# Sliding and dilated attention with a squared-ReLU block: v without overlapping key blocks, halos copied by ScalarE, larger DMA rows for dilated q k and for the results

## The chip, the cores and the metric

The kernel runs on one NeuronCore of a Trainium2 chip, as one launch. The metric is the device time of that launch in microseconds (us). The core has five engines that run their own instruction queues in order: TensorE (PE, matmuls, with its weight loads shown as PEld), VectorE (DVE), ScalarE (ACT), GpSimd (POOL) and SyncE (SP). DMA transfers are issued here from SP and from POOL.

## The reference

```python
# q, k, v: (8 batches, 8 heads, 576 positions, 64) float32
scores = scale * np.matmul(q, k.transpose(0, 1, 3, 2))
rel = pos[:, None] - pos[None, :]
mask_plain = (rel >= 0) & (rel < 32)                          # heads 0-3
mask_dil = (rel >= 0) & (rel < 32 * 4) & (rel % 4 == 0)       # heads 4-7
attn = softmax(where(mask, scores, -1e9))
x = np.matmul(attn, v).transpose(0, 2, 1, 3).reshape(4608, 512)
g = np.maximum(x @ w_in, 0.0) ** 2                            # w_in: 512 x 2048
out = g @ w_out                                               # w_out: 2048 x 512
```

A query of a sliding head (0 to 3) sees itself and the 31 positions before it. A query of a dilated head (4 to 7) sees every fourth position, 32 in all; sorted by position modulo 4 (a "class"), it is again a window of 32 within its class of 144.

## The kernel before

**Attention, per batch.** The sliding heads work in 6 blocks of QB = 96 queries, each against 128 keys: its own 96 and the PADP = 32 before them. The dilated heads work per class in 2 blocks of QD = 72 queries, each against 128 keys: its own 72 and the PADD = 56 before them. `s_sliding` and `s_dilated` compute scores as keys x queries into PSUM; `softmax` takes the exponential on ACT (L509) into `AT` and multiplies with a 0/1 mask on DVE (L510, `maskp` and `maskd`). `av_sliding` and `av_dilated` multiply `AT` with v (L567, L581), where a column of ones beside v gives the sum of the row; `normalize` divides on DVE (L552, L553). `x_sliding` and `x_dilated` transpose the result on PE, and ACT copies it into `xT` (L602, L620).

**v.** Since every key block has 128 rows and the blocks overlap, v is loaded with the overlap: `load_sliding_v` (L124) issues six DMAs from SP into `sv` (float32, 128 partitions, blocks outermost), each with the block's 32 rows of halo; `load_dilated_v` (L133) issues two into `sd`, of 72 and of 128 rows. POOL then casts them to float16 (`cast_sliding_v` L166, three copies; `cast_dilated_v` L170, four copies) into `vp` and `vd`, of which there are two each, for even and odd batches. For batch 0 two small DVE copies (L662, L664) stand before the loads, so that these start after the q k loads; for batch 1 two POOL copies (L687, L688) do that. `sv` and `sd` exist once.

**q and k.** For batches 0 and 1 they are loaded by POOL's DMAs (`load_qk`) and transposed on PE (`t_sliding`, `t_dilated`). From batch 2 on the DMA engines transpose. Sliding: load (`load_sliding_qk`), re-ordering copy `nr` (`by_token`, L119, on POOL for batch 2, on DVE afterwards), a store to a DRAM tile `dp` (L194), transposes from there into `QKTp` (L202). Dilated: a copy from DRAM to DRAM with a cast to float16 into `dd` (`keep_dilated_qk`, L183), whose rows are padded from 256 to 320 elements, and transposes from there into `QKTd` (L206). Before the loads for the next batch POOL waits for the transposes (`after_transposes`, L211).

**Hidden layer and output.** The 4608 tokens are worked in 9 chunks of 512. `mm1_gen` makes 16 hidden blocks per chunk: 4 matmuls (L269), Relu on ACT into `rt` (L292), square on DVE into `g` (L293). Chunks 0 and 1 use plain products (`mm2`, L403). Chunks 2 to 8 use one level of Strassen (`mm2_strassen_gen`): seven products of half width, whose operands DVE prepares as sums (`gs` L302 and L303, `g` L372, `wt` L319). ACT takes a product out of PSUM (`take`, L359), DVE adds another one (`add`, L370), and SP stores each of the four 256x256 quarters of the chunk with its own DMA (`leave`, L362), in rows of 1 KB.

**The order** is written by hand. The attention of batch b is emitted step by step, and between its steps `pump(n)` emits n pieces of the hidden layer of chunk b - 1, so PE, ACT and DVE each see attention and hidden layer interleaved in a fixed order. `attn_scores` and `attn_values` hold the steps; hooks in them emit the transfers for the next batch. Batch 0 is written out at L661 to L712, with filler matmuls (`fill_gen`) between its steps.

Of the kernel before, what the change touches and what calls it, by code (L numbers as in the profile page):

```python
# [17 lines left out]
def kernel(  # L18
# [32 lines left out]
    PADD = P - QD  # L51
    KPAD = 64
    DPAD = 64
# [9 lines left out]
    otp = ctx.enter_context(tc.tile_pool(name="otp", bufs=5))  # L63
# [27 lines left out]
    sv = stg.tile([P, NB, HH, D], FP32, name="sv")  # L91
# [32 lines left out]
    def load_sliding_v(b):  # L124
        for m in range(NB):
            lo = QB * m - PADP
            p0 = PADP if m == 0 else 0
            nc.sync.dma_start(
                out=sv[p0:P, m, :, :],
                in_=v[b, 0:HH, lo + p0 : lo + P, :].transpose([1, 0, 2]),  # L130
            )

    def load_dilated_v(b, eng):  # L133
        vv = v[b, HH:H].rearrange("h (i c) d -> i h (c d)", c=DIL)
        eng.dma_start(out=sd[PADD:P, 0, :, :], in_=vv[0:QD])
        eng.dma_start(out=sd[:, 1, :, :], in_=vv[QD - PADD : CL])

# [28 lines left out]
    def cast_sliding_v(b, ms=range(0, NB, 2)):  # L166
        for m in ms:
            nc.gpsimd.tensor_copy(vp[b % 2][:, m : m + 2, :, 0:D], sv[:, m : m + 2, :, :])  # L168

    def cast_dilated_v(b):  # L170
        for t in range(2):
            for c in range(0, DIL, 2):
                nc.gpsimd.tensor_copy(  # L173
                    vd[b % 2][:, t, c : c + 2, :, 0:D],
                    sd[:, t, :, D * c : D * (c + 2)].rearrange("p h (c d) -> p c h d", d=D),
                )

# [5 lines left out]
    def keep_dilated_qk(b):  # L183
        d = dpool.tile([2, HH * CL, DIL * D + DPAD], FP16, name=f"dd{b}", tag="dd")
        for i, src in ((1, k), (0, q)):
            nc.gpsimd.dma_start(
                out=d[i, :, 0 : DIL * D], in_=src[b, HH:H].rearrange("h (i c) d -> (h i) (c d)", c=DIL)
# [16 lines left out]
    def transpose_dilated(b, dd):  # L204
        for i in (1, 0):
            nc.sync.dma_start_transpose(out=QKTd[b % 2][:, i, :, KPAD:], in_=dd[i, :, 0 : DIL * D])  # L206
# [10 lines left out]
    nc.vector.memset(sv[0:PADP, 0, :, :], 0.0)  # L217
# [12 lines left out]
    for m, w, pad in ((maskp, QB, PADP), (maskd, QD, PADD)):  # L230
# [7 lines left out]
            m.rearrange("p (n w) -> p n w", w=w),  # L238
            lo_[:, 0:w].unsqueeze(1).to_broadcast([P, UW // w, w]),
            hi_[:, 0:w].unsqueeze(1).to_broadcast([P, UW // w, w]),  # L240
        )
    nc.vector.memset(AT[:, :, UW:640], 0.0)
    for r in range(2):
# [8 lines left out]
            scalar1=-PADD + 0.5,  # L252
# [71 lines left out]
    def mm2_strassen_gen(c, g):  # L324
# [32 lines left out]
        def take(what):  # L357
            ot = otp.tile([P, 2, HM], FP32, name=f"o{what}{c}", tag="ot")
# [3 lines left out]
        def leave(ot, i, j):  # L362
            t0 = c * TOKC + HTOK * i
            nc.sync.dma_start(
                out=out[t0 : t0 + HTOK, HM * j : HM * (j + 1)].rearrange("(t p) m -> p t m", p=P),
                in_=ot,
# [4 lines left out]

        nc.vector.tensor_sub(g[:, 0:HF, HTOK:], g[:, 0:HF, 0:HTOK], g[:, 0:HF, HTOK:])  # L372
        yield from product(A, gq(0, 0), wq(0, 0))
        o11 = take("u")
# [4 lines left out]
        o21 = take("v")  # L379
# [5 lines left out]
        o22 = take("w")  # L385
        add(o22, Bk)
        leave(o22, 1, 1)
# [3 lines left out]
        leave(o11, 0, 0)  # L391
        yield
        yield from product(A, sq(1), wq(1, 1))
        o12 = take("x")
        leave(o12, 0, 1)
# [3 lines left out]
        leave(o21, 1, 0)  # L399
# [10 lines left out]

    def store(c, t, po):
        ot = otp.tile([P, DM], FP32, name=f"ot{c}_{t}", tag="ot")
# [116 lines left out]
    def s_dilated(b, g):  # L529
        tiles = [pa(f"pz{b}_{g}_{h}") for h in range(2)]  # L530
        for h, ps in enumerate(tiles):
            for a in range(2):
                for t in range(2):
                    q0 = KPAD + (2 * g + h) * CL + QD * t
                    for e in range(2):
# [4 lines left out]
                            QKTd[b % 2][r, 1, a, q0 - PADD : q0 - PADD + P],  # L540
# [84 lines left out]
    def attn_scores(b, gap, less=0, hooks={}):  # L625
# [5 lines left out]
        for g in range(2):  # L631
            s_dilated(b, g)
            if 2 + g in hooks:
                hooks[2 + g]()
            pump(gap - less)

    def attn_values(b, gap, wide=False, hooks={}):
        xs = []
        for mp in range(3):
            xs.append(av_sliding(b, mp))  # L640
            if 4 + mp in hooks:
                hooks[4 + mp]()
            pump(gap)
        x_sliding(b, 0, xs, wide)
        pump(gap)
# [151 lines left out]
```

## Time and profile before

| what | value |
|---|---|
| median of 11 runs | 315.65 us (313.05 to 318.95) |
| the profiled execution | 316.13 us |
| its span, first to last instruction | 314.1 us |
| granted TensorE clock | 1.000 |
| PE busy | 291.6 us (93%) |
| DVE busy | 210.2 us (67%) |
| ACT busy | 165.0 us (53%) |
| POOL busy | 76.4 us (24%) |
| DMA | 82801 packets, 46.73 MB, mean 149 GB/s |
| DMA packets under 512 B | 54352 |
| loads of v | sv 40 x 128 KB and 8 x 96 KB, sd 8 x 512 KB and 8 x 288 KB |

A line of the profile names the line of the code, the engine, the operation, and "out<-in" by the names of the tiles. In a timeline the first column is the start and the second the busy time in us; "x2" says how many instructions were merged; the bracket at the end tells how long the engine was idle before and what ended that. In a list of waits the numbers are the total in us, how many times, and the longest. A busy PE is not always PE at full rate, since its matmuls are pipelined and may wait inside.

### The profile page before, as it was taken

To read this page: it belongs to the slowest core of one execution; us is meant where nothing else is said; L and a number is where in the kernel's file an instruction comes from. 1 tells how busy PE (TensorE), PEld (TensorE's weight loads), DVE (VectorE), ACT (ScalarE), POOL (GpSimd) and SP (SyncE) were. 2 spreads that over 40 slices of the span, in tenths; PEclk is the share of its full clock that TensorE was granted. 3 is DMA by queue.
4 is the path that set the end of the run, shared out by engine and by line. 5 is a ranking of instruction groups with operands and counts; after the bars stand their busy time and mean duration, and the time that the engine had idled before them with its cause. 6 is when DMAs were issued, how large, how long until landed. Compare 5 with 4: busy or idle time off the path is not lost.

```text
span 314.1 us, 7145 instructions
## 1 busy us (share of the span) xinstructions
PE 291.6 (93%) x2874; PEld 195.4 (62%) x2874; DVE 210.2 (67%) x429; ACT 165.0 (53%) x286; POOL 76.4 (24%) x114
## 2 busy tenths in 40 slices
PE   1878998996999989998999999999999999999994
PEld 1444554453555558755798968557845885685583
DVE  5774448476852899479937993799469944734652
ACT  2736645566535942495239623872287336525620
POOL 4444018403320657022530514060000000000000
PEclk9999999999999999999999999999999999999999
DMA  7799997999999998999689977987310030012003
GB/s 125 160 228 214 205 201 130 195 192 205 206 172 201 293 219 159 229 179 222 168 171 215 247 150 101 261 203 151 102 35 0 2 102 33 0 38 100 3 0 134
DMA packets 82801, 46.73 MB, mean 149 GB/s; under 512 B 54352, under 2 KB 79952, under 8 KB 82768
## 3 DMA queue, kind: packets, MB, share of 16 engines
q1 hardware_dynamic: 68512, 31.60, 43.2%
q0 software_dynamic: 14256, 14.68, 28.8%
q8 instruction: 22, 0.36, 0.5%
q14 instruction: 11, 0.09, 0.1%
HBM read 39.85 MB, written 16.52 MB: 179 GB/s over the span
## 4 chain that ended last, share of the span: by engine, by line
PE 61%; DVE 19%; DMA 7%; ACT 5%; issue 2%; SPq 2%; POOL 1%; POOLq 0%; DVEq 0%
PE ph L269 24%; PE pa L346 12%; PE po L403 8%; PE pb L346 7%; DVE g L293 5%; ACT AT L509 3%; PE pc L346 3%; DVE x_p L553 3%; DMA sd<-in_v_dram 3%; DMA ns<-in_q_dram 2%; DVE AT L510 2%; DVE gs L303 2%; ACT rt L292 2%; DVE gs L302 2%; PE paw L581 2%
## 5 line engine op out<-in xcount | busy, mean ns | idle before, releaser
L269 PE MATMUL ph<-xT,wi 128*128 128x512 f16 (+1 forms) x640 | 133.4, 359 | 0.7 <-ACT xT L620 0.7
L292 ACT ACTIVATE rt<-ph 128x512 f16<-128x512 f32 x144 | 86.2, 615 | 45.4 <-PE ph L269 40.1
L269 PEld LDWEIGHTS <-wi 128*128 128x128 f16 x640 | 68.6, 114 | 46.8 <-issue 0.8
L293 DVE TENSOR_TENSOR g<-rt 128x512 f16<-128x512 f16 x144 | 64.1, 453 | 42.4 <-ACT rt L292 41.3
L346 PEld LDWEIGHTS <-g 128*128 128x128 f16 x448 | 42.3, 98 | 7.1 <-DVE g L372 1.4
L168 POOL CAST vp<-sv 128x512 f16<-128x512 f32 x24 | 17.1, 712 | 82.9 <-DMA sv<-in_v_dram 58.7
L346 PEld LDWEIGHTS <-gs 128*128 128x128 f16 x336 | 31.4, 98 | 5.4 <-DVE gs L303 2.0
L403 PE MATMUL po<-wo,g 128*128 128x512 f16 x128 | 33.1, 379 | 0.0
L173 POOL CAST vd<-sd 128x512 f16<-128x512 f32 x32 | 27.8, 905 | 11.4 <-DMA sd<-in_v_dram 8.9
L346 PE MATMUL pa<-wt,gs 128*128 128x256 f16 x224 | 29.1, 273 | 0.9 <-DVE gs L303 0.6
L346 PE MATMUL pb<-wt,g 128*128 128x256 f16 x224 | 27.7, 273 | 0.6 <-DVE g L372 0.6
L553 DVE TENSOR_TENSOR x_d<-paw,rcp_d 72x512 f16<-72x512 f32 x32 | 22.0, 686 | 1.1
L509 ACT ACTIVATE AT<-pz 128x576 f16<-128x576 f32 x32 | 20.0, 710 | 2.2 <-PE pz L538 2.0
L510 DVE TENSOR_TENSOR AT<-AT,maskp 128x576 f16<-128x576 f16 x32 | 16.4, 521 | 7.0 <-ACT AT L509 4.9
L509 ACT ACTIVATE AT<-ps 128x576 f16<-128x576 f32 x32 | 19.2, 661 | 3.4 <-PE ps L519 3.3
L620 ACT COPY xT<-py 128x576 f16<-128x576 f16 x16 | 10.2, 641 | 17.2 <-PE py L614 17.0
L510 DVE TENSOR_TENSOR AT<-AT,maskd 128x576 f16<-128x576 f16 x32 | 17.0, 548 | 3.1 <-ACT AT L509 1.5
L602 ACT COPY xT<-px 128x576 f16<-128x576 f16 x16 | 10.2, 639 | 14.3 <-PE px L596 13.7
L370 DVE TENSOR_TENSOR ov<-pb,ov 128x512 f32<-128x512 f32 x7 | 4.8, 692 | 18.2 <-PE pb L346 18.2
L553 DVE TENSOR_TENSOR x_p<-pav,rcp_p 96x512 f16<-96x512 f32 x24 | 16.5, 687 | 0.8
L581 PEld LDWEIGHTS <-AT 128*128 128x128 f16 x256 | 11.7, 98 | 6.7 <-issue 1.7
L403 PEld LDWEIGHTS <-g 128*128 128x128 f16 x128 | 10.4, 98 | 8.0
(81 smaller groups left out, 284.6 us busy)
## 6 DMA issues: line engine op xcount, KB each, us to landing
sv<-in_v_dram SPq DMA_DIRECT2D x40, 128.0 KB, 6.5
sd<-in_v_dram SPq DMA_DIRECT2D x8, 512.0 KB, 7.3
dp<-nr SPq DMA_DIRECT2D x12, 288.0 KB, 5.1
ns<-in_k_dram POOLq DMA_DIRECT2D x8, 288.0 KB, 5.4
ns<-in_q_dram POOLq DMA_DIRECT2D x8, 288.0 KB, 6.9
sd<-in_v_dram SPq DMA_DIRECT2D x8, 288.0 KB
wo<-in_moe_w_out_dram POOLq DMA_DIRECT2D x4, 512.0 KB, 10.2
out_dram<-ow SPq DMA_DIRECT2D x7, 256.0 KB
```

Of the source, the lines that this page charges most:

```text
L168: nc.gpsimd.tensor_copy(vp[b % 2][:, m : m + 2, :, 0:D], sv[:, m : m + 2, :, :])
L173: nc.gpsimd.tensor_copy(vd[b % 2][:, t, c : c + 2, :, 0:D], sd[:, t, :, D * c : D * (c + 2)].rearrange("p h (c d) -> p c h d", d=D),)
L269: nc.tensor.matmul(ph[:, t0:t1], wi4[ffc // 4][:, dmk, :, ffc % 4], xT[:, dmk, x0 : x0 + t1 - t0], start=(dmk == 0 and t0 == 0), stop=(dmk ...
L292: nc.scalar.activation(rt, ph[:], ACTF.Relu)
L293: nc.vector.tensor_mul(g[:, ffc, :], rt, rt)
L346: nc.tensor.matmul(banks[bank][:, t], a(k, t), b(k), start=(new and t == 0 and k == 0), stop=(k == HF - 1), skip_group_check=True,)
L403: nc.tensor.matmul(po, g[:, ffc, t * P : (t + 1) * P], wo[ffc // 4][:, ffc % 4, :], start=(ffc == 0), stop=(ffc == NFF - 1),)
L509: nc.scalar.activation(AT[:, u, 0:UW], ps[:, :, 0 : UW // 2], ACTF.Exp, scale=scale)
L510: nc.vector.tensor_mul(AT[:, u, 0:UW], AT[:, u, 0:UW], mask)
L553: nc.vector.tensor_tensor(out=x[0:w], in0=pv[:, :, :, 0:D], in1=rcp[0:w].unsqueeze(3).to_broadcast([w, 2, HH, D]), op=ALU.mult,)
L581: nc.tensor.matmul(pav[:, e, h * (D + 2) : h * (D + 2) + D + 1], AT[:, 4 + h, off : off + P], vd[b % 2][:, t, 2 * a + e, h, 0 : D + 1], st ...
L602: nc.scalar.copy(xT[:, 0:2, t0 : t0 + 288], px[:, 0:UW].rearrange("x (c t) -> x c t", c=2),)
```

## The change

It has three parts.

1. v is loaded without overlap. A sliding block loads only its own 96 rows, into partitions 32 to 127 of `sv`, whose layout is now head, block, element; from batch 1 on this takes two DMAs (two heads each) instead of six. The dilated heads now have key blocks of 80 and 64 own rows (`OWND`), and the padding differs per block (`PADD = (48, 56)`), so each of two DMAs loads own rows only. POOL casts as before (the second dilated block on 64 partitions only). What the overlap brought is then copied on chip by ACT, from the end of one block to the start of the next: `halo_sliding` (three per batch, 32 partitions, 256, 512 and 512 elements) and `halo_dilated` (two per batch, 64 partitions, 512 elements). They stand in ACT's order behind the dilated scores and between the steps of `attn_values`. The rows of `sv` that no DMA writes any more are set to 0 once, by one more memset on DVE ahead of L662; `maskd` is made in two halves, since its two blocks differ.
2. `dd` has no padding any more, and the copy into it reads 16 positions (4 KB) at a time and writes 2 KB, where it read 1 KB and wrote 512 B.
3. The two quarters of the same tokens share a tile of full width, and `leave` stores both in one DMA with 2-KB rows; the last chunk still stores quarters. The pool of these tiles has 3 buffers of twice the size instead of 5.

```diff
-    PADD = P - QD
+    PADD = (48, P - QD)
+    OWND = (CL - 64, 64)
...
-    otp = ctx.enter_context(tc.tile_pool(name="otp", bufs=5))
+    otp = ctx.enter_context(tc.tile_pool(name="otp", bufs=3))
...
-    sv = stg.tile([P, NB, HH, D], FP32, name="sv")
+    sv = stg.tile([P, HH, NB, D], FP32, name="sv")
...
     def load_sliding_v(b):
-        for m in range(NB):
-            lo = QB * m - PADP
-            p0 = PADP if m == 0 else 0
-            nc.sync.dma_start(
-                out=sv[p0:P, m, :, :],
-                in_=v[b, 0:HH, lo + p0 : lo + P, :].transpose([1, 0, 2]),
-            )
+        vv = v[b, 0:HH].rearrange("h (m p) d -> p h m d", p=QB)
+        if b == 0:
+            for m in range(NB):
+                nc.sync.dma_start(out=sv[PADP:P, :, m, :], in_=vv[:, :, m, :])
+        else:
+            for h in (0, 2):
+                nc.sync.dma_start(out=sv[PADP:P, h : h + 2], in_=vv[:, h : h + 2])
...
     def load_dilated_v(b, eng):
         vv = v[b, HH:H].rearrange("h (i c) d -> i h (c d)", c=DIL)
-        eng.dma_start(out=sd[PADD:P, 0, :, :], in_=vv[0:QD])
-        eng.dma_start(out=sd[:, 1, :, :], in_=vv[QD - PADD : CL])
+        i0 = 0
+        for t in range(2):
+            eng.dma_start(out=sd[P - OWND[t] : P, t, :, :], in_=vv[i0 : i0 + OWND[t]])
+            i0 += OWND[t]
...
+    def halo_sliding(b, mp):
+        m0, m1 = max(1, 2 * mp), 2 * mp + 2
+        nc.scalar.copy(
+            vp[b % 2][0:PADP, m0:m1, :, 0:D], vp[b % 2][P - PADP : P, m0 - 1 : m1 - 1, :, 0:D]
+        )
+
+    def halo_dilated(b, c):
+        nc.scalar.copy(
+            vd[b % 2][0:64, 1, c : c + 2, :, 0:D], vd[b % 2][64:P, 0, c : c + 2, :, 0:D]
+        )
...
-        d = dpool.tile([2, HH * CL, DIL * D + DPAD], FP16, name=f"dd{b}", tag="dd")
+        d = dpool.tile([2, HH * CL, DIL * D], FP16, name=f"dd{b}", tag="dd")
         for i, src in ((1, k), (0, q)):
             nc.gpsimd.dma_start(
-                out=d[i, :, 0 : DIL * D], in_=src[b, HH:H].rearrange("h (i c) d -> (h i) (c d)", c=DIL)
+                out=d[i].rearrange("(r i) x -> r (i x)", i=4),
+                in_=src[b, HH:H].rearrange("h (r i) d -> (h r) (i d)", i=16),
+                max_dma_last_dim=4096,
             )
...
-    for m, w, pad in ((maskp, QB, PADP), (maskd, QD, PADD)):
+    md = maskd.rearrange("p (n t w) -> p n t w", t=2, w=QD)
+    for m, w, pad in (
+        (maskp.rearrange("p (n w) -> p n w", w=QB), QB, PADP),
+        (md[:, :, 0], QD, PADD[0]),
+        (md[:, :, 1], QD, PADD[1]),
+    ):
...
+    nc.vector.memset(sv[0:PADP, :, 1:NB, :], 0.0)
     nc.vector.memset(AT[:, :, UW:640], 0.0)
...
         take(upper, 1)
-        leave(o12, 0, 1)
+        leave(upper, 0, (1,) if last else (0, 1))
...
             s_dilated(b, g)
             if 2 + g in hooks:
                 hooks[2 + g]()
+            if g:
+                halo_sliding(b, 0)
             pump(gap - less)
...
             xs.append(av_sliding(b, mp))
+            if mp < 2:
+                halo_sliding(b, mp + 1)
+            else:
+                halo_dilated(b, 0)
...
         x_sliding(b, 0, xs, wide)
+        halo_dilated(b, 2)
         pump(gap)
```

In batch 0, which is written out, `halo_sliding(0, 0)` stands behind the sliding scores and ahead of `t_dilated`, `halo_sliding(0, 1)` behind `t_dilated`, and the other three behind the dilated scores.

## The prediction

> **What bounds the kernel now.** I read the page, then PE's waits, the busy time by stage, and the order of time at three places. PE is busy 291.6 of the 314.1 us span. So I first ask where PE waits at all. In the list of waits for PE alone (us in total, times, longest), these three matter:
>
> ```profile
> PE pav L567 <- DVE x_p L553: 2.8, 3, 1.5
> PE ps L519 <- DMA QKTp<-dp: 2.5, 1, 2.5
> PE paw L581 <- POOL vd L173: 1.6, 1, 1.6
> ...
> ```
>
> After the start-up nothing else reaches 1 us, so less DMA traffic can only buy these few waits. The stages confirm it (us, then PE, PEld, DVE, ACT, POOL busy; clock; DMA share; GB/s):
>
> ```profile
> 62.00:97.00 35.00, 32.52 (x270) 17.28 (x269) 21.81 (x47) 18.92 (x33) 8.02 (x14) 1.00 1.06 189
> 97.00:131.00 34.00, 32.28 (x323) 22.27 (x322) 26.00 (x48) 18.91 (x34) 15.93 (x19) 1.00 1.01 219
> 162.50:195.00 32.50, 31.78 (x382) 28.13 (x381) 24.98 (x49) 17.86 (x32) 10.28 (x14) 1.00 0.93 176
> 227.00:258.00 31.00, 31.00 (x319) 21.91 (x318) 22.79 (x48) 17.86 (x32) 0.00 (x0) 1.00 0.11 36
> ```
>
> The DMA engines are full up to about 195 us, but the stage with almost no DMA still takes 31.0 us, all of it PE. The middle stages are only 0.5 to 3 us above that. From 258 us on PE never waits, and that part is not changed except for wider stores.
>
> **Start-up, to the first full matmul of the hidden layer at 25.75 us.**
>
> ```profile
> 7.36 0.16 DVE L664 CAST sd<-ns 64x2 f32<-64x2 f16 x1
> 7.47 3.80 SPq L128 DMA_DIRECT2D sv<-in_v_dram  x6
> 7.54 1.42 DVE L164 COPY QKTp<-pt 128x576 f16<-128x576 f16 x2
> ...
> 13.58 0.38 SPq L136 DMA_DIRECT2D sd<-in_v_dram  x1
> ...
> 21.79 1.18 POOL L173 CAST vd<-sd 128x512 f16<-128x512 f32 x2 [3.14 <-DMA sd<-in_v_dram]
> ...
> 25.75 1.46 PE L269 MATMUL ph<-xT,wi 128*128 128x512 f16 x6 [0.73 <-ACT xT L620]
> ```
>
> DVE works without a pause from 4.08 us to these copies, and both the v load (gated by L662 and L664) and the scores (which need QKTp) stand behind it. The change puts more there: a memset of sv over 1280 elements of 32 partitions, and the dilated mask in two halves. The memset rows are 0.27 us for 256 elements and 0.91 us for 1024, so 0.83 ns an element and 1.13 us. The maskd triple (L231, L234, L237) took 0.80 us; two triples of half width come to about 2 x 0.62 = 1.24, so 0.44 more. Everything behind moves by 1.57 us. Bounds: 0 if a transfer turns out to be what the scores wait for, 2.0 us if the halves cost like whole masks.
>
> Against this, v(0) is 1152 KB instead of 1536 KB. The second dilated piece falls from 512 to 256 KB; it was issued at 13.58 and landed 8.15 us later, beside the 2 MB (as stored) of wi. Even started 1.57 us later it should land by 20 us. Then the cast wait (1.6 us on PE, 1.13 us on DVE) goes, and what is late next is DVE's row of x_d, at its own pace. Worth about 1.1 us. The first ACT halo stands ahead of ACT's two QKTd copies and waits for POOL's cast of the first two key blocks; the DVE halves of those copies ended 0.4 us after ACT's (13.88 against 13.47), which covers its 0.4 us. The second fits in ACT's 1.0 us gap before the dilated exps. The other three stand before the xT copies, whose reader (mm1) is later. Start-up net: **+0.5 us** (-1.0 to +2.5).
>
> **Batch 2, the 2.5 us wait of PE at 74.77 us.**
>
> ```profile
> 54.09 0.66 POOL L186 DMA_DIRECT2D dd<-in_q_dram  x1
> 57.84 2.11 POOL L119 COPY nr<-ns 128x2304 f16<-128x2304 f16 x1 [3.08 <-DMA ns<-in_q_dram]
> 62.68 6.85 SPq L206 DMA_TRANSPOSE QKTd<-dd  x2
> 69.63 3.14 SPq L202 DMA_TRANSPOSE QKTp<-dp  x2
> ...
> 74.77 0.43 PE L519 MATMUL ps<-QKTp 64*128 64x96 f16 x12 [2.48 <-DMA QKTp<-dp]
> ```
>
> SP issues the dilated transposes first, and the second of them starts at 66.20, about when dd of q lands (12 us after its issue); the sliding ones queue behind. Two parts of the change shorten this. POOL issues ns(2) and dd(2) only after its v(1) casts, which end at 52.2 and hang on v(1) landing. Up to there the queues carry 2 x 384 KB less, at 205 GB/s 3.7 us. And dd itself: the trace's packet records have 1152 packets of 512 B a batch at 61 ns, over 16 engines 4.4 us; the new copy writes 288 of 2 KB, and 2-KB packets of that queue took 174 ns, so 3.1 us. QKTp should be there 4 to 5 us earlier and the whole wait go. At 72.3 us PE has its next operands, and DVE was idle too, so nothing takes its place: **-2.4 us** (0 to -2.5). POOL's v casts stay as long: the dilated ones already read a permuted sd at the same 611 ns minimum as the sliding ones, and 64 partitions cost like 128.
>
> The padding of dd goes too (rows of 512 instead of 640 B). Here the row comes first: dp has unpadded 512-B rows, and its transposes land in 3.7 us, dd's padded ones in 3.8. A rule of the Trainium skill, "DMA: Bandwidth & Descriptors", section "Latency and other measured facts", speaks against it: row pitches at large powers of two fall from 207 to 103 GB/s, and padding brings the rate back. If that held here, each dilated transpose would take some 7.6 us and batch 2 keep its wait (2.4 us lost). The rule was measured from 512 KiB pitch up, and dp's row is near: I take nothing.
>
> **The other DMA waits.** In chunk 3 DVE stood 0.99 us at 141.59 for ns of batch 5, and PE then waited 1.0 us on x_p. That load runs beside v(5), now a quarter smaller, and follows dd and the transposes: -0.8 us (0 to -1.0). In chunk 2 PE's 1.5 us at 115.5 comes from DVE, whose mask multiplies took 1.65 us for two beside POOL's casts, and 1.00 elsewhere. The casts come some 3 us earlier, but the next batch's move into the same stretch: -0.5 us (+0.5 to -1.5). Stores in 2-KB rows: 6 x 1024 packets at 59 ns become 3072 at 85, some 1 us of DMA time a chunk; nobody waits for a store, and three otp buffers of twice the size are reused 12 us or more after their store is issued: 0.
>
> **What is added: five ACT copies a batch.** No row has ACT copying SBUF to SBUF. The nearest are COPY out<-PSUM 128x512 at 587 ns and 128x576 at 640: 0.83 ns an element, so 0.59 us for 512 and 0.38 for 256, in all 2.7 us a batch, 22 us of ACT. Bounds 0.45 (a shorter start on SBUF) and 0.735 us (the re-ordering copy QKTd<-pd). The sum by average says nothing (ACT is at 53%); the place does, in the stage where PE never waits:
>
> ```profile
> 237.23 1.22 ACT L292 ACTIVATE rt<-ph 128x512 f16<-128x512 f32 x2
> ...
> 238.82 0.60 ACT L292 ACTIVATE rt<-ph 128x512 f16<-128x512 f32 x1 [0.37 <-PE ph L269]
> ...
> 239.06 0.42 PE L567 MATMUL pav<-vp,AT 128*128 128x65 f16 x8
> ```
>
> ACT is gapless to 238.45. The halo for blocks 0 and 1 goes in at 237.25, ends at 237.6, and only the second half of the first pav (from 237.7) needs it: no wait. The two rt then end at 238.8, the next halo at 239.4, and its pav wants to start at 239.06: PE waits 0.4 us. Queued behind it is the next rt, and behind that DVE's g; the third halo ends at 240.6, before its pav. The rt of the last two hidden blocks come some 0.5 us later; gs, which needs them, had 0.68 us of room (246.42 against 247.10). So +0.4 in chunk 6; in chunks 2 to 5 the same wait is partly covered, since PE later waits for DVE anyway: 0.25 each; batch 1 about 0.2, batch 2, where ACT has room, 0.1. Sum **+1.7 us** (0.5 to 6).
>
> **Sum.** 0.5 - 2.4 - 0.8 - 0.5 + 1.7 = -1.5, say -1.4 us. The profiled execution took 316.13 us (span 314.1 and 2.0 around it), so 314.7 there; the median of the runs, 315.65, is 0.5 lower: **314.2 us**. A difference of 0.5%, 1.6 us, is about what can be told from none.
>
> **Rivals.** *More comes free* (0.27): start-up gains 1.0 us since the DVE delay is absorbed, and all waits for DVE shrink with the earlier casts: 1.0 + 2.4 + 1.0 + 1.2, less 1.1 for ACT, is -4.5: 311.1 us. For it: by the packet records the change saves 5120 packets of 256 B at 21.6 ns, 1792 of 1 KB at 59 ns, and the dd and store shares above, some 27 us over 16 engines, of the 226 us (72% of the span) that both queues take. Against it: DVE's work is not less.
>
> *ACT becomes late* (0.20), slower. The halos take 0.735 us or more and push rt, so DVE's g and gs come late where PE already waits for gs (0.5 us in chunk 4). Each of chunks 2 to 5 then pays 0.5 at pav and 0.5 at gs, chunk 6 pays 1.2, batches 1 and 2 0.8: 6.0 instead of 1.7, so 318.5 us. It outweighs all gains once the halos cost over 3.1 us of PE in all. Against it: idle ACT of 0.27 to 0.52 us before most rt.
>
> *Nothing nets* (0.08): the dd copies land no earlier, because their reads share full queues, and batch 2 keeps its wait; 2.4 lost of the gains, with ACT at its lower bound (1.2 less): -0.2, 315.5 us.
>
> The forecast has 0.45. About half of it lies over 0.5% faster: faster 0.46, within 0.34, slower 0.20. The range 310.8 to 317.9 takes in the first rival and the start-up's upper bound and leaves out most of the late-ACT case.
>
> **What would show it.** Right: no PE wait on QKTp at batch 2, dd landing well under 8.8 and 11.0 us, halos near 0.59 us, the first full ph at 26.2 us, and a wait of pav on an ACT copy of some 0.3 us a chunk. Wrong: halos over 0.7 us; a stage without DMA longer than 31.6 us; first ph after 27.5 us; POOL's casts of v(2) so late that a halo holds up ACT.

## The result and the profile after

The change made the kernel slower: 319.39 us in the median of 12 runs (318.44 to 322.17) against 315.42 for the kernel before (47 runs, 312.40 to 319.38). The ratio is 1.015, with a 95% interval of 1.0124 to 1.0175. The forecast was 314.2 us with a range up to 317.9, so the change went the other way, and further than the range.

The profiled execution took 318.55 us, with a span of 316.8 (before: 316.13 and 314.1). The two profiled executions are thus 2.4 us apart where the medians are 4.0 apart: the profile after is one of its kernel's fastest executions, the one before lies above its median. What the two profiles show is some two thirds of the loss. Every ratio here is made from the undisturbed runs of both kernels on the same chip, those within 1.5% of the fastest of their kernel, so it need not be the quotient of two medians, and for two kernels, named below, only an execution of 604.0 and one of 764.6 us was profiled, from which nothing is read of PE.

The page is as foreseen where it speaks of amounts: DMA packets fell from 82801 to 67024, bytes from 46.73 to 43.58 MB, ScalarE's busy time rose from 165.0 to 184.0 us. PE's list of waits is where the time went (us in total, times, longest):

```profile
PE ps L556 <- DVE QKTp L166: 2.5, 1, 2.5
PE pav L604 <- DVE x_p L590: 2.3, 2, 1.1
PE pa L370 <- DVE gs L327: 1.8, 2, 1.1
PE pav L604 <- ACT vp L185: 1.3, 6, 0.5
...
PE pav L604 <- ACT rt L316: 1.0, 1, 1.0
```

The wait for QKTp by a DMA, 2.5 us before, has gone, and so has the one on POOL's vd. In their place PE waits for DVE: at the start-up for the first QKTp (0.6 before, 2.5 now), and later for x_p and gs. ScalarE's halos (vp L185) hold PE for 1.3 us in six small waits.

The stages that answer to those shown of before, each from one chunk's first full ph to the next one's (us, then PE, PEld, DVE, ACT, POOL busy; clock; DMA share; GB/s):

```profile
63.60:96.80 33.20, 32.77 (x270) 17.14 (x269) 23.47 (x47) 21.22 (x38) 9.36 (x14) 1.00 0.96 186
96.80:131.30 34.50, 32.49 (x323) 22.30 (x322) 26.83 (x48) 21.31 (x39) 12.79 (x19) 1.00 0.99 188
164.70:197.00 32.30, 31.84 (x382) 28.37 (x380) 24.77 (x49) 20.11 (x37) 8.08 (x12) 1.00 0.93 178
229.30:260.60 31.30, 31.14 (x318) 21.94 (x317) 22.81 (x47) 20.00 (x37) 0.00 (x0) 1.00 0.10 37
```

PE, DVE and ACT run the same stages as before with a little more on ACT (about 2.2 us a chunk). To see where the lag builds up, I compared the start of one and the same PE instruction, the first full ph of each chunk, in every kernel. The table gives what each stage added (+) or saved against before, in us of the profiled executions. PE runs the same order of matmuls in all of them (fillers aside). The sum is the lag at the start of chunk 7. A star marks a stage in which the granted clock fell to half for 3.4 us, which by itself costs up to half of that, 1.7 us (last section). Every row is one execution: that of part 1 alone took 323.57 us, 5.1 above its kernel's median, that of parts 2 and 3 alone 316.42, 2.4 above.

```
kernel                      start   c0     c1     c2     c3     c4     c5     c6    sum
after                       +1.66   0.0   -1.80  +0.51  +1.82  -0.20  +0.34  +0.37  +2.7
part 1 alone                +1.74   0.0   +2.71* +0.84  +2.23  -0.18  +0.25  +0.36  +7.9
parts 2 and 3 alone         -0.48   0.0   +1.25* +0.21  -0.26  +0.42  -0.47   0.0   +0.65
after, no halos             +2.29  -0.44  +1.09* +0.47  +2.27   0.0   +0.36   0.0   +6.1
after, memset early         +0.89   0.0   -0.93  +0.28  +1.84  -0.08  +0.58  +0.36  +2.9
after, six loads            +1.23   0.0   -0.99  +2.30* -0.39  +0.13   0.0   +0.37  +2.6
after, nr later             +1.72  +0.58  -1.12  +0.19  -0.55  -0.23  +0.13  +0.36  +1.1
after, start-up rearranged  +0.25  +1.66* -1.36  +0.19  +2.01  +0.05  +0.57  +0.37  +3.7
parts 2 and 3, mended       +0.99  +1.25* -2.54  -0.44  -0.55   0.0   -0.47   0.0   -1.8
all mended, no halos        +0.48  -0.42  -2.55  +0.73  -0.96   0.0   +0.07   0.0   -2.7
parts 2 and 3, mended, fill -0.87  -0.16  -0.54  -0.56  -0.55  +0.31  -0.31   0.0   -2.7
```

In the profile after, the start-up (+1.66) and chunk 3 (+1.82) are most of the loss, chunk 1 is the gain, and the halos add about 0.35 where nothing else disturbs (chunk 6).

The start-up, in order of time:

```profile
6.82 1.12 DVE L265 MEMSET sv<- 32x1280 f32 x1 [0.20 <-issue]
9.35 3.00 SPq L128 DMA_DIRECT2D sv<-in_v_dram  x6
9.42 1.42 DVE L166 COPY QKTp<-pt 128x576 f16<-128x576 f16 x2
13.22 2.13 PE L536 MATMUL pd<-ident,nd 128*128 128x128 f16 x18
13.48 0.40 ACT L185 COPY vp<-vp 32x256 f16<-32x256 f16 x1
14.42 0.73 ACT L164 COPY QKTd<-pd 128x512 f16<-128x512 f16 x1 [0.54 <-PE pd L536]
17.99 2.96 POOL L178 CAST vd<-sd 128x512 f16<-128x512 f32 x4 [0.76 <-DMA sd<-in_v_dram]
18.27 2.21 DVE L547 TENSOR_TENSOR AT<-AT,maskd 128x576 f16<-128x576 f16 x3 [0.20 <-ACT AT L546]
22.59 0.69 DVE L590 TENSOR_TENSOR x_d<-paw,rcp_d 72x512 f16<-72x512 f32 x1
27.41 0.81 PE L293 MATMUL ph<-xT,wi 128*128 128x512 f16 x3 [0.73 <-ACT xT L657]
```

and in the kernel before:

```profile
11.34 1.27 PE L499 MATMUL pd<-ident,nd 128*128 128x128 f16 x18
15.17 2.43 DVE L510 TENSOR_TENSOR AT<-AT,maskd 128x576 f16<-128x576 f16 x4 [0.43 <-ACT AT L509]
19.71 0.69 DVE L553 TENSOR_TENSOR x_d<-paw,rcp_d 72x512 f16<-72x512 f32 x1
```

DVE reaches QKTp at 9.42 instead of 7.54. On the way to the first x_d the lag grows from 1.88 to 2.88 us. The casts of vd no longer stand still for the second piece of sd (3.14 us before), as foreseen, which takes 1.22 us back, and the first full ph is at 27.41 instead of 25.75.

Chunk 3, with the loads for batch 5:

```profile
132.40 2.61 SPq L131 DMA_DIRECT2D sv<-in_v_dram  x2
134.14 0.62 POOL L111 DMA_DIRECT2D ns<-in_q_dram  x1
135.12 4.67 SPq L137 DMA_DIRECT2D sd<-in_v_dram  x2
142.75 0.76 DVE L119 COPY nr<-ns 128x2304 f16<-128x2304 f16 x1 [1.81 <-DMA ns<-in_q_dram]
145.16 0.41 PE L604 MATMUL pav<-vp,AT 128*128 128x65 f16 x8 [1.05 <-ACT rt L316]
147.35 2.59 POOL L170 CAST vp<-sv 128x512 f16<-128x512 f32 x3 [11.50 <-DMA sv<-in_v_dram]
149.48 2.23 DVE L317 TENSOR_TENSOR g<-rt 128x512 f16<-128x512 f16 x3
153.81 1.05 PE L370 MATMUL pa<-wt,gs 128*128 128x256 f16 x8 [1.06 <-DVE gs L327]
```

and in the kernel before:

```profile
133.03 6.92 SPq L128 DMA_DIRECT2D sv<-in_v_dram  x6
133.87 0.63 POOL L111 DMA_DIRECT2D ns<-in_q_dram  x1
140.04 2.21 SPq L135 DMA_DIRECT2D sd<-in_v_dram  x1
141.59 0.76 DVE L119 COPY nr<-ns 128x2304 f16<-128x2304 f16 x1 [0.99 <-DMA ns<-in_q_dram]
148.61 1.24 DVE L293 TENSOR_TENSOR g<-rt 128x512 f16<-128x512 f16 x3
```

SP has issued all of v(5) by 139.8. In the kernel before the six loads of sv took 6.92 us to issue (133.03 to 139.95) and sd followed only at 140.04 to 143.8. So now all of v is issued while ns is in flight, and ns of q lands 8.6 us after its issue instead of 7.7. The other profiles agree: 8.5 to 9.1 us in the six kernels that load sv in two DMAs, 7.0 to 7.7 in the six that do it in six. DVE stands at nr for 1.81 us (0.99 before). Behind nr on DVE's queue wait g and x_p, behind these ScalarE's rt (for g) and PE's third pav. POOL's three casts of sv, spread from 141.9 to 148.9 before, now wait for the whole load and run in one bunch from 147.35, with the vd casts behind them, beside DVE's g and gs: the three g at 149.5 take 2.23 us (1.24 before), and PE waits 1.06 us for gs. Of the 1.82 us PE loses 0.31 at the first halo, only 0.09 at the third pav (where it also stood before the change, for x_p), and 1.41 behind it, at pc and pa, which wait for g and gs.

### The profile page after: what moved, and what is told of

Same layout as the page of the kernel before. It is cut to its first block, busy times and chain, and to the rows that moved or that the text cites. A ratio compares the mean times of both kernels' runs of the same rounds, so it can differ in the third digit from the quotient of the medians.

```text
span 316.8 us, 7107 instructions
## 1 busy us (share of the span) xinstructions
PE 293.5 (93%) x2874; PEld 196.5 (62%) x2874; DVE 215.5 (68%) x433; ACT 184.0 (58%) x326; POOL 73.0 (23%) x114
## 2 busy tenths in 40 slices
DMA packets 67024, 43.58 MB, mean 138 GB/s; under 512 B 48624, under 2 KB 59376, under 8 KB 66992
## 4 chain that ended last, share of the span: by engine, by line
PE 59%; DVE 19%; DMA 7%; ACT 7%; issue 3%; SPq 2%; POOL 1%; DVEq 0%; POOLq 0%
PE ph L293 21%; PE pa L370 13%; PE pb L370 8%; PE po L436 7%; DMA ns<-in_q_dram 5%; DVE g L317 5%; ACT AT L546 4%; PE pc L370 3%; DVE AT L547 3%; DVE x_p L590 3%; ACT rt L316 2%; PE paw L618 2%; DVE gs L326 2%; DVE gs L327 1%; PE pf L490 1%
## 5 line engine op out<-in xcount | busy, mean ns | idle before, releaser
L316 ACT ACTIVATE rt<-ph 128x512 f16<-128x512 f32 x144 | 85.1, 603 | 36.8 <-PE ph L293 34.5
L317 DVE TENSOR_TENSOR g<-rt 128x512 f16<-128x512 f16 x144 | 66.5, 469 | 42.8 <-ACT rt L316 41.8
L370 PEld LDWEIGHTS <-g 128*128 128x128 f16 x448 | 42.3, 98 | 6.9 <-DVE g L401 0.9
L397 DVE TENSOR_TENSOR ov<-pb,ov 128x512 f32<-128x512 f32 x14 | 9.7, 692 | 29.5 <-PE pb L370 18.2
L386 ACT COPY ov<-pa 128x512 f32<-128x512 f32 x14 | 8.2, 585 | 29.5 <-PE pa L370 29.5
L178 POOL CAST vd<-sd 128x512 f16<-128x512 f32 (+1 forms) x32 | 24.4, 790 | 2.6 <-DMA sd<-in_v_dram 2.0
L547 DVE TENSOR_TENSOR AT<-AT,maskp 128x576 f16<-128x576 f16 x32 | 17.6, 567 | 4.1 <-ACT AT L546 2.3
L604 PEld LDWEIGHTS <-AT 128*128 128x128 f16 x192 | 9.2, 98 | 12.4 <-issue 8.9
L386 ACT COPY ou<-pa 128x512 f32<-128x512 f32 x14 | 8.2, 588 | 14.7 <-PE pa L370 14.7
```

The source lines that it names most:

```text
L178: nc.gpsimd.tensor_copy(vd[b % 2][p0:P, t, c : c + 2, :, 0:D], sd[p0:P, t, :, D * c : D * (c + 2)].rearrange("p h (c d) -> p c h d", d=D),)
L316: nc.scalar.activation(rt, ph[:], ACTF.Relu)
L317: nc.vector.tensor_mul(g[:, ffc, :], rt, rt)
L370: nc.tensor.matmul(banks[bank][:, t], a(k, t), b(k), start=(new and t == 0 and k == 0), stop=(k == HF - 1), skip_group_check=True,)
L386: nc.scalar.copy(ot, banks[A])
L547: nc.vector.tensor_mul(AT[:, u, 0:UW], AT[:, u, 0:UW], mask)
```

## Experiments

The theory after reading the two traces: the loss is all in part 1, and it is in orders of work rather than in amounts: DVE's queue at the start-up, the two big loads of v, and, smallest, the halos. The rivals: the halos on ScalarE are the main cost; or the dd copies or wide stores hurt.

**Part 1 alone, and parts 2 and 3 alone.** The kernel before with one part of the change, taken over as in the diff above.

> Part 1 of the change alone (v without overlap, the halos on ScalarE, the masks in halves, the memset of sv); dd padded and stores in quarters as before. The whole change costs about +4 us in the medians (+2.7 in the profiled spans). Theory (all of the loss is in part 1: +1.7 at the start-up, some +2.5 from v's two big loads with their late casts, about +1 from the halos, and only the lighter traffic of part 2 takes back the wait at batch 2): this kernel takes 319.5 to 321.5 us, at least as long as the whole change, with the first full ph at 27.4 us and a wait of PE on QKTp at batch 2 of 1 us or more. Rival (the dd copy or the wide stores hurt, for instance by delaying the loads that share the queues): clearly below the whole change, 316 to 317.5 us.

> Parts 2 and 3 alone (dd copied in 4-KB reads without padding, results in 2-KB rows); v, masks and start-up as before. Theory (parts 2 and 3 are harmless or help): 313 to 315.5 us against 315.5 before, first full ph at 25.75 us, the 2.5 us wait of PE on QKTp at batch 2 gone or half as long. Rival (these two hurt): 317 us or more, with the loss spread over chunks 2 to 5, where dd is copied and results are stored.

Measured: part 1 alone 318.47 us, ratio 1.0125 (1.0085 to 1.0165); parts 2 and 3 alone 314.04 us, ratio 0.9967 (0.9941 to 0.9993). So the loss is in part 1, and parts 2 and 3 are a small gain; the rival that they hurt falls. Part 1 alone came out 1 us below its expected range and not above the whole change; the two intervals overlap, so no more is read from that. Nor do the parts add up (+1.25% and -0.33%, against +1.5% for the whole); the rest is about as large as the intervals and stays open. The wait of PE for QKTp at batch 2 is 2.1 us with parts 2 and 3 alone, where the theory had it gone or half as long; with part 1 alone it is 3.4, in that long execution.

**The halos left out.**

```diff
     def halo_sliding(b, mp):
         m0, m1 = max(1, 2 * mp), 2 * mp + 2
-        nc.scalar.copy(
-            vp[b % 2][0:PADP, m0:m1, :, 0:D], vp[b % 2][P - PADP : P, m0 - 1 : m1 - 1, :, 0:D]
-        )
     def halo_dilated(b, c):
-        nc.scalar.copy(
-            vd[b % 2][0:64, 1, c : c + 2, :, 0:D], vd[b % 2][64:P, 0, c : c + 2, :, 0:D]
-        )
+        return
...
     for r in range(2):
+        nc.gpsimd.memset(vd[r][0:64, 1, :, :, 0:D], 0.0)
```

> The whole change without its five ScalarE copies a batch; this leaves the halo out of the computation (the keys ahead of a block count as zero in the values). Theory (halos are the smallest of the three costs, about 1 us in all): 317.5 to 318.7 us, start-up still 27 us or more to the first full ph, chunks 2 to 5 as slow as with the change. Rival (the halos on ScalarE are the main cost): 315 to 316 us, back at the time before, with chunk 3 at 32.8 us instead of 34.6.

Measured: 321.03 us, ratio 1.0188 (1.0138 to 1.0238), no faster than with the halos (the intervals overlap). Neither theory had that. The table says why it is no measure of the halos: the POOL memset that the experiment needed (1.95 us from 4.54) runs beside DVE's work on the masks, where one instruction takes 1.03 us instead of 0.20, so that DVE's memset of sv starts at 7.81 instead of 6.82, and the start-up is 0.6 us longer; and at batch 2 PE waits again 2.0 us, after which its clock falls to half (the starred 1.09). Where nothing of that reaches, the halos can be read: chunk 6, +0.37 with halos, is 0.0 without. That the halos are the main cost is refuted all the same, by chunk 3, which is as slow without them (+2.27). A cleaner run follows below.

**The memset moved, and the whole start-up of DVE rearranged.** First only the memset of sv goes to where DVE waits for its first inputs; then the dilated mask also moves behind QKTp's copies.

```diff
     nc.vector.memset(sd[0:64, 0, :, :], 0.0)
+    nc.vector.memset(sv[0:PADP, :, 1:NB, :], 0.0)
...
-    nc.vector.memset(sv[0:PADP, :, 1:NB, :], 0.0)
     nc.vector.memset(AT[:, :, UW:640], 0.0)
```

> The whole change with one instruction moved: the 1.12-us memset of sv stands ahead of the masks, where DVE waits for its first inputs. Theory (DVE's extra work ahead of QKTp and of the gate of v is the start-up's loss of 1.7 us): the first full ph comes 0.9 to 1.2 us earlier, at 26.3 us, and the time is 1 us less than the whole change, about 318.3 us. Rival (the start-up hangs on v's transfers or on the halos ahead of the QKTd copies): ph stays within 0.3 us of 27.4 and the time that of the whole change.

> The whole change with DVE's start-up rearranged: the memset of sv stands where DVE waits for its first inputs, and the dilated mask is made behind the QKTp copies, half of it between the softmax steps and half behind the QKTd copies. Theory (the order of DVE's queue sets the start-up): QKTp's copies start at 6.9 us or earlier, the first full ph comes at 26 us or earlier (27.4 with the change, 25.75 before), and the time is 1.5 us less than the whole change. With the memset alone moved ph came at 26.65. Rival (the halos ahead of the QKTd copies and the waits for v's casts hold the start-up): ph stays at 26.6 us or later.

Measured: the memset alone moved 320.06 us, ratio 1.0185 (1.0136 to 1.0234); all rearranged 318.45 us, ratio 1.0106 (1.0061 to 1.015). As a mechanism the theory holds in the main: the first full ph comes at 26.65 us with the memset moved and at 26.01 with all rearranged, against 26.99 to 27.50 in the four profiles with the start-up of the change, so some 1 to 1.4 of the 1.66 us hang on DVE's order. QKTp's copies start at 8.56, not at 6.9 as expected, since DVE then waits 1.40 us for ns of q. As a time it fell short: moving the memset shows nothing in the median, and with all rearranged it is 0.9 us less, with intervals that overlap. In its profile the start-up lost what it had won at once, in the half clock of the starred chunk 0; the other five executions have a mean clock of 0.997 and more and still a median of 318.30, so that is not the reason.

**Six loads instead of two, and nr later.** Two ways to keep DVE from standing at nr in chunk 3.

```diff
-        if b == 0:
-            for m in range(NB):
-                nc.sync.dma_start(out=sv[PADP:P, :, m, :], in_=vv[:, :, m, :])
-        else:
-            for h in (0, 2):
-                nc.sync.dma_start(out=sv[PADP:P, h : h + 2], in_=vv[:, h : h + 2])
+        for m in range(NB):
+            nc.sync.dma_start(out=sv[PADP:P, :, m, :], in_=vv[:, :, m, :])
```

```diff
-            hooks[{3: 6}.get(b, 3)] = turn
+            hooks[{3: 6, 4: 6}.get(b, 3)] = turn
```

> The whole change, but from batch 1 on v of the sliding heads comes in six DMAs, one a block (96 rows, still no overlap), instead of two of two heads each. Theory (with two big DMAs all of v's packets are in the queues at once, so ns of batch 5 lands 1 us later and DVE, stuck at the copy nr<-ns, holds x_p and with it PE; and POOL can cast nothing until all of sv is there): in chunk 3 DVE's wait for ns falls from 1.8 to 1 us or less, POOL's first cast of v(5) comes some 4 us earlier, the chunk takes 33 us instead of 34.6, and the time is 1.5 us less than the whole change, about 318 us. Rival (chunk 3's loss is the halos', or chance): chunk 3 stays at 34 to 35 us and the time does not move.

> The whole change, but in chunk 3 the step that copies ns into nr, stores it and issues the transposes for batch 5 is emitted three steps later (where chunk 2 has it), so that DVE does not stand at it before ns has landed. Theory (DVE's queue stuck behind that copy is what makes chunk 3 1.8 us longer): no wait of DVE for ns, PE's waits on x_p and rt at the third pav of chunk 3 gone, chunk 3 at 32.5 to 33 us instead of 34.6, the time 1.5 to 2 us less than the whole change. Rival (the halos on ScalarE, or POOL's bunched casts beside DVE, make the chunk long): chunk 3 stays above 34 us. A risk for both: the transposes for batch 5 start later and PE may wait for them in chunk 4.

Measured: six loads 317.47 us, ratio 1.009 (1.0061 to 1.0119); nr later 316.97 us, ratio 1.0067 (1.0031 to 1.0103). Against the whole change that is 1.9 and 2.4 us, about half of the loss each. Chunk 3 with six loads, in order of time:

```profile
133.79 6.46 SPq L127 DMA_DIRECT2D sv<-in_v_dram  x6
135.86 0.63 POOL L111 DMA_DIRECT2D ns<-in_q_dram  x1
140.35 3.71 SPq L133 DMA_DIRECT2D sd<-in_v_dram  x2
142.70 0.89 POOL L166 CAST vp<-sv 128x512 f16<-128x512 f32 x1 [5.12 <-ACT AT L542]
143.59 0.76 DVE L119 COPY nr<-ns 128x2304 f16<-128x2304 f16 x1 [0.47 <-DMA ns<-in_q_dram]
```

The bytes are the same as with two loads. What changed is the pace: SP needs 6.46 us to issue the six, sd starts at 140.35, ns lands 7.7 us after its issue again, DVE waits 0.47 us, and the first cast comes 4.7 us earlier. The chunk is 0.4 us shorter than before the change. (In this profile chunk 2 lost 2.30 us, by a wait of 2.3 us for x_p and the half clock behind it, so its sum is no better than that of the change; the gain in time is read from the medians.) With nr later, v still comes in two loads and ns still takes 8.7 us, but DVE reaches the copy only when it is long there:

```profile
133.21 2.31 SPq L131 DMA_DIRECT2D sv<-in_v_dram  x2
135.00 0.63 POOL L111 DMA_DIRECT2D ns<-in_q_dram  x1
148.21 0.74 DVE L119 COPY nr<-ns 128x2304 f16<-128x2304 f16 x1
```

No bracket stands behind nr: it waits for nothing. Chunk 3 is 0.55 us shorter than before the change, and chunk 4, with the later transposes, is not longer. The theory of chunk 3 holds in both of its links: without the crowding by the big loads, or without DVE standing in front of it, the 1.8 us are gone, with the halos still on ScalarE. And with nr later POOL's casts still run in one bunch (148.21 to 156.1), so the bunch alone does not make the loss.

**Parts 2 and 3 with the two orders mended.** v as in the kernel before; the dilated mask behind QKTp's copies and nr later.

```diff
-    for m, w, pad in ((maskp, QB, PADP), (maskd, QD, PADD)):
+    bounds(lo_, hi_, QB, PADP)
+    band(maskp, lo_, hi_, QB)
...
+    bounds(lo_d, hi_d, QD, PADD)
     pending.append(fill_gen())
     for hp in range(2):
         s_sliding(0, hp)
+        if hp == 0:
+            band(maskd, lo_d, hi_d, QD)
         pump(1)
...
-            hooks[{3: 6}.get(b, 3)] = turn
+            hooks[{3: 6, 4: 6}.get(b, 3)] = turn
```

`bounds` makes lo and hi, `band` their product, as the loop did.

> Not the change: parts 2 and 3 alone (v as before, no halos), with two things rearranged: the whole dilated mask is made behind the QKTp copies, in DVE's gaps between the softmax steps, and the step with nr of chunk 3 stands three steps later. Theory (both are places where DVE's order, not its work, sets PE's time): first full ph at 25 us or earlier, no wait of DVE for ns or of PE for x_p in chunk 3, some 1.5 to 2.5 us less than parts 2 and 3 alone, which had 314.0: about 312 us. Rival (PE waits elsewhere instead, for v's casts at the start-up or for the later transposes in chunk 4): 313.5 to 315 us.

Measured: 312.63 us, ratio 0.9923 (0.989 to 0.9955): faster than both kernels, by about 2.5 us against before. In the profile chunk 3 has no wait for ns. The first full ph, however, came at 26.74, later than before the change: it had to wait for ns of q at PE's first transposes (2.7 us instead of 1.1 in the list of waits), a transfer that this edit does not touch, and again the clock fell to half just behind it.

**All mended, with and without halos, and the halos on POOL.** The whole change with six loads, nr later, the start-up rearranged, and two pairs of filler matmuls between the last steps of batch 0. Then the same without halos, the POOL memset now where POOL is idle; then with the halos of batches 1 to 7 as POOL copies behind their casts.

```diff
     begun = [mm1_begin(0, 0)]
+    fill = fill_gen("e")
+    next(fill)
     zs.append(av_dilated(0, 1, 1))
...
     x_dilated(0, 1, zs, False)
+    next(fill)
```

```diff
             nc.gpsimd.tensor_copy(
                 vp[b % 2][:, m : m + 2, :, 0:D], sv[:, :, m : m + 2, :].rearrange("p h m d -> p m h d")
             )
+            if b:
+                halo_sliding(b, m // 2, True)
...
```

The last diff shows one place of several: the copies for vd go behind their casts in the same way, and those on ScalarE go from batch 1 on.

> The whole change with all that helped it: v of the sliding heads in six DMAs (317.5 alone), the step with nr of chunk 3 later (317.0 alone), DVE's start-up rearranged (318.45 alone), and two small filler matmul pairs on PE between the last steps of batch 0. Theory (the loss was in three orders of work, not in loading v without overlap): the gains add in part, 314 to 315.5 us, below or at the kernel before; what is left over parts 2 and 3 mended (312.6) is the halos' cost of about 0.3 us a chunk in chunks 2, 4, 5 and 6. Rival (loading v without overlap costs by itself, through ScalarE's copies and the time of POOL's casts): 316 us or more.

> The kernel of e9 without its ScalarE halo copies; this leaves the halo out of the computation (the keys ahead of a block count as zero in the values). The earlier kernel without halos had also got a memset on POOL ahead of DVE's ones and so a later start; here that stands where POOL is idle. Theory (the halos cost some 0.3 us of PE in four chunks and little elsewhere): 1 to 1.7 us less than e9, and no wait of PE for a ScalarE copy into vp. Rival (halos cost nothing, the slower run without them was no accident): the time of e9 within 0.5 us.

> The kernel of e9 with the halos of batches 1 to 7 on POOL, each right behind the casts that it reads. Theory (POOL is idle three quarters of the time and runs these copies long before they are needed): the waits of PE for halos go, 1 us less than e9. Rival (POOL's copies run beside DVE's and make it slower, as its casts do, and end the cast of the last v later): as e9 or up to 2 us more, with more waits of PE for x_p and gs.

Measured on one chip: all mended 315.00 us, ratio 1.0007 (0.9975 to 1.004); without halos 314.19 us, ratio 0.9988 (0.9952 to 1.0024); halos on POOL 321.14 us, ratio 1.0202 (1.014 to 1.0264). The first and the third are the two without a usable profile. With three orders mended the change is 4.4 us faster and level with the kernel before, so most of the loss was in the orders. But not all of it: the kernel to set beside it is the next one, which has the same mended orders and fillers and the old loads of v, and takes 312.68 us on the same chip, with an interval that does not touch this one. Loading v without overlap thus still costs 2.3 us, and the rival keeps that part. The halos are worth 0.8 us of it, as the difference of two medians whose intervals overlap, less than the theory's 1 to 1.7; the theory that the halos are all that is left fails. And POOL is the worst place for them: about 6 us more than on ScalarE. All its executions but the profiled one have a mean granted clock of 0.989 to 0.995, as only one of 20 has with the halos on ScalarE, so a part of the 6 us is PE at half clock, which follows PE's waits (last section). What PE waits for there (slower DVE beside POOL, later casts, as expected) has no usable trace behind it and stays an argument.

**Parts 2 and 3 mended, with the fillers.** The kernel of 312.63 us and the first of the two diffs above.

> Parts 2 and 3 alone, mended as in e8 (v as before, no halos), and the two filler pairs of e9. Theory (in the profiled execution of e8 PE's clock fell to half for 3.4 us at 27.0 us, since PE had stood idle 1.5 us of the 3.4 us before; fillers keep it busy, which is worth up to 1.7 us in those executions that show the drop): no clock drop at the start-up, 311.5 to 312.3 us in the median against 312.6. Rival (fillers only push the last steps of batch 0 back, or the drop moves elsewhere): 312.6 to 313.5 us.

Measured: 312.68 us, ratio 0.9936 (0.991 to 0.9961). In the profile the clock does not fall at the start-up any more and the first full ph is at 24.88 us, but the median is the same within 0.1 us: the fillers bring no gain that these runs can tell. On the same chip this kernel, with overlapping v, is 1.5 us below the mended change without halos. Their two profiled executions end level (-2.7 both), so where this 1.5 us lies stays open; the table has the non-overlapping v 1.35 us later at the start-up, 2 us better in chunk 1, and 1.3 us worse in chunk 2.

## Why the prediction was wrong

In the terms of the table the forecast is -1.5 and the profiles give +2.7. Of the 4.2 us between them 2.4 are in chunk 3, 1.2 at the start-up, 0.8 in chunk 2 and 0.5 in chunk 1; the other chunks came out 0.6 better.

**Start-up: the delay mis-sized, 1.57 against 2.88, and so +0.5 against +1.66.** Ahead of QKTp DVE lost 1.88: the memset took 1.12 (forecast 1.13), with 0.2 of idle time ahead of it, and the rest is in the mask halves, whose multiply took 0.31 us each where a whole one took 0.46. Two delays behind that the prediction did not have. The 18 transposes of q and k (pd) took 2.13 us instead of 1.27: PE's clock rose to full at 15.59, where it had risen at 11.54 before, and PE's first pav is late by 2.44 us. Then the last multiply with the dilated mask took 0.86 us instead of 0.46, beside POOL's casts of vd. That makes 2.88 us at the first x_d. From there the credit for the vanished vd wait came as forecast, 1.22 us for 1.1. The first halo was covered, as forecast: it ended at 13.88, and ScalarE then still stood 0.54 us for PE's pd (0.57 before). The third one was not free, as counted: PE's pav at 20.08 waits 0.16 us for it. Much here is one execution's: with nr later, which changes nothing at the start-up, the clock rose at 13.52 and pd was fast, but v landed late, ScalarE's second halo stood 1.10 us for POOL's cast, and the start came out the same (+1.72).

**Batch 2: the number right, by luck.** -2.4 was forecast, and the profile has -2.54 between the ph ahead of the wait and the ps behind it, which waits for nothing:

```profile
73.86 0.43 PE L556 MATMUL ps<-QKTp 64*128 64x96 f16 x12
```

But QKTp was to be there 4 to 5 us earlier, and it landed at 73.54 instead of 74.63, 1.1 us earlier. The rest of the wait is gone because PE itself came there 1.6 us later, with the loss of the start-up. The 12 us that the prediction read for dd of q were not of this place: there it took 7.3 us before and takes 7.5 now (the medians over all batches fell, from 8.8 and 11.0 us to 6.6 and 8.2). In the six other kernels with the lighter v and dd QKTp landed between 71.19 and 76.01, and five of them kept a wait: 0.6 to 1.3 us (start-up rearranged, memset early, nr later, six loads), and 2.0 in the first one without halos. And of the 2.54 us chunk 1 gave 0.75 back at its second and third pav. That the profiled execution of the change was a lucky one here would explain the 1.3 us or so by which the medians differ more than the profiles; it was not shown, since the other executions have no trace.

**Chunk 3: the step that failed most.** The prediction said of ns of batch 5: "That load runs beside v(5), now a quarter smaller, and follows dd and the transposes: -0.8 us". Measured: +1.82. The bytes were counted and the issue was not. With fewer, larger DMAs the last of v was issued some 4 us earlier (139.8 instead of 143.8), while ns was still on its way (134.1 to 142.7), and ns came 0.9 us later instead of earlier; DVE stood in front of it, and g and gs behind. Six loads of the same bytes bring the chunk back to -0.39, and nr three steps later to -0.55. Set against -0.8 and 0.25 for the halo, this chunk alone is 2.4 us off.

**Chunk 2: wrong sign, -0.5 (and 0.25 for the halo) against +0.51.** In the profile 0.31 us are lost at the first pav, with its halo, 0.35 gained at the third (PE waits 1.1 us for x_p instead of 1.5), and 0.54 lost at pa, which waits 0.7 us for gs instead of 0.2. The casts did come earlier, as argued: those of vd, which started at 118.42, now run from 114.02 to 117.13. But there they stand beside DVE's last four g, which take 2.69 us instead of 1.74. With nr later or the start-up rearranged the chunk was +0.19 with the casts at the same place; I have no run that settles this half microsecond.

**Halos: right mechanism, oversized.** The durations were forecast at 0.59 and 0.38 and measured at 0.60 and 0.40. In chunk 6 the cost is +0.37 (forecast 0.4), but at another halo. The prediction let the first one start at 237.25, where the rt behind the dilated exps had started; it started when the exps had ended, 0.25 later in that count, and so came too late for the second half of its pav:

```profile
239.79 0.40 ACT L185 COPY vp<-vp 32x256 f16<-32x256 f16 x1
239.80 0.29 PE L604 MATMUL pav<-vp,AT 128*128 128x65 f16 x4
...
240.25 0.29 PE L604 MATMUL pav<-vp,AT 128*128 128x65 f16 x4 [0.15 <-ACT vp L185]
```

The first pav is split in two fours around the wait for the halo: 0.58 us from its start to the next ph (240.38), where a whole pav behind (241.72 to 241.98) takes 0.26. The second halo, on which the forecast's wait was put, costs nothing, since PE now comes later. In all the halos cost 0.8 us by the medians of the mended kernels, where 1.7 was forecast. So the rival that ended slower, "ACT becomes late", had a time near the result for a wrong reason: it wanted halos of 0.735 us and 0.5 us of waiting both at pav and at gs in each of chunks 2 to 5.

**Nothing for the stores and the padding: right.** Parts 2 and 3 together gained 0.3%. Transposes from unpadded dd landed in 4.0 us (3.8 before), so nothing like a halved rate is seen at rows of 512 bytes. The rule that the prediction weighed did not fit the case in any event: in the row of the Trainium skill, "DMA: Bandwidth & Descriptors", section "Latency and other measured facts", a padding of 4 KiB brought the rate back and one of 192 bytes did not, and dd's padding was 128 bytes. POOL's casts stayed as long, as forecast: 0.79 us on 64 partitions as on 128.

## What to carry to other kernels

When a change merges or splits DMAs, work out when each one is issued as well as how many bytes it moves: here a queue that needed 7 us to issue six loads paced them, and without it what loaded beside them came 0.9 us later. An instruction that waits for a DMA in the middle of an in-order engine's queue (here DVE's nr) turns a microsecond of landing time into waits of three engines; emitting it three steps later cost nothing here and was worth 2.4 us. A gain that rests on a transfer landing just in time, like that of batch 2, should be counted with the lateness of whoever waits for it. And one-time set-up instructions belong where the engine waits for its first inputs: in the profiles that moved the first full ph forward by 1 to 1.4 us, though the medians did not show it.

## What the runs showed of the hardware

PE's clock fell to half for one stretch of 3.41 us in six of the profiled executions. These stretches begin a multiple of 3.41 us after the clock first rose. The two stretches around PE's wait for QKTp at batch 2, parts 2 and 3 alone (us, PE, PEld, DVE, ACT, POOL busy; clock; DMA share; GB/s):

```profile
70.59:74.00 3.41, 1.29 (x11) 0.54 (x11) 2.00 (x5) 1.30 (x3) 0.18 (x1) 1.00 1.01 203
74.00:77.41 3.41, 3.41 (x19) 1.36 (x18) 1.58 (x4) 1.79 (x3) 2.52 (x5) 0.50 0.96 169
```

and in the kernel before:

```profile
72.98:76.39 3.41, 1.62 (x18) 1.02 (x19) 0.99 (x4) 1.28 (x3) 1.66 (x4) 1.00 0.96 216
76.39:79.80 3.41, 3.41 (x42) 1.66 (x40) 3.41 (x7) 3.11 (x7) 1.06 (x2) 1.00 1.01 162
```

In the first, PE was busy 1.29 of 3.41 us and then ran at clock 0.50: its full ph started every 0.43 us there, and every 0.22 behind. In the second it was busy 1.62 us, its wait of 2.48 us lying across two such stretches, and kept its clock. In these runs idle times of 2.01 to 3.35 us in one stretch of dense work brought the drop (four times), 1.87 and less did not; at the start-up, with its small matmuls, 1.5 us was enough (the mended start-ups). The Trainium skill, "TensorE: Matmul & The Clock Gate", section "HAM oscillation — how this bites in real kernels", tells to avoid idle gaps over about 3.4 us; here a gap of 2.0 us was enough where it lay within one stretch, and the measurement decides. A wait of PE thus costs either itself or itself and up to 1.7 us, by where it falls. That is part of why the runs of one kernel spread by 4 to 7 us: of 31 runs of the kernel before on one chip, 24 have a mean granted clock of 0.997 or more and a median of 314.53 us, and 7 have 0.995 or less and 317.22. It is no part of the change's loss: all of its 12 runs have 0.997 or more.
